# A fused attention and feed-forward kernel: the hand-written order of all engines replaced by another order

## The chip, the cores and the metric

The kernel runs on one core of a Trainium2 chip. The metric is the device time of one execution in microseconds (us). The core has four engines that compute, and each works through its own queue in order: PE (TensorE, matrix products and transposes), ACT (ScalarE), DVE (VectorE) and POOL (GpSimd). A fifth, SP (SyncE), issues all the transfers between the chip's memory (HBM) and the on-chip buffers. An engine that reaches an instruction whose input or buffer isn't ready waits there, with everything that stands behind it in its queue.

## The reference

There are B = 4 batches of N = 12480 tokens with C = 128 features, and m = 32 inducing vectors. A batch is read twice: the inducing vectors attend to all its tokens, which gives a 32 x 128 matrix h; then every token attends to the 32 rows of h. All 49920 results go through a feed-forward part.

```python
def mab(q, kv):
    s = scale * (q @ kv.transpose(0, 2, 1))
    s = s - s.max(-1, keepdims=True)
    a = np.exp(s)
    a /= a.sum(-1, keepdims=True) + 1e-09
    return a @ kv
h = mab(I, x)
return mab(x, h).astype(np.float32)
...
h = x @ w_in          # 128 -> 2048
g = h - np.tanh(h)
return (g @ w_out).astype(np.float32)
```

## The kernel before, in words

A batch is cut into seven steps of 1792 tokens, numbered (b, s) with s from 0 to 6; a step is one transfer of 896 KB each way. Two steps that follow each other form a pair (their group g is 0 to 3; the last group has one step).

The first pass (`first`, L276) does for each step: SP loads the transposed tokens (L286); PE multiplies them with the inducing vectors (the scores, L274); DVE copies a pair of steps out of the accumulator PSUM and takes the maximum (L298). When all seven steps are there, the maximum is spread (L309 to L314), ACT takes the exponentials pair by pair (L323) and DVE transposes them in blocks (L325). PE then sums exponentials times tokens (L356), for which the tokens are needed in their untransposed form. Eleven of the 28 steps load that form as well (L334, the set `LOADED`); for the other 17 PE transposes the tokens in two halves (L344), and ACT or DVE copies each half out of PSUM (L350 and L351; the copies run in a helper, L167 on ACT and L169 on DVE). A batch ends with small products that give h (L362 to L381).

`linear` (L385) replaces the feed-forward part by a tangent around the mean of the 32 rows of h, so that the feed-forward part and the second attention become one 32 x 128 matrix per batch. The second pass (`second`, L458) computes the scores of each token against h (L274 again), copies them out and takes a maximum (L477), takes exponentials (L499), and multiplies with that matrix (L507); the result of a step comes in two halves, each moved out of PSUM by ACT (L523) or DVE (L525) with a scale and an offset, and SP stores the step (L514). The last two steps of batch 3 are stored in halves.

`bound` (L540) works out at the end whether the tangent is accurate enough: a product (L580), a choice of rows (L586), `least` on DVE (L590), a transpose on PE (L603), `gather` (L607) and `decide` (L615), which writes one number. After that all five engines load that number (L696) and branch on it (L697); for these inputs the general path is skipped.

The weights come as 64-bit numbers in eight pieces of 512 KB (L233) and are turned into float32 by four instructions on DVE and two on ACT per piece (L236 to L257).

`IDLE` matrix products (L219) compute nothing that is used.

Nothing is scheduled by a compiler. `add` numbers each operation in the order of the program text, and the string `ORDER` (L42) lists all numbers again in the order in which they are issued. The letter behind a number chooses the engine (P, A, D, S, G), which matters for the operations that are declared `ACT/DVE`. The small letters behind it choose a place for each buffer that the operation uses first: 19 places for 896 KB steps (`big`), 3 PSUM places of two banks (`d`), and so on (`PLACES`, L36). A buffer's first writer waits until the place's former user is done; for a place that held a result, that is the landing of its store.

Of the kernel before, what the change touches and what calls it, by code (L numbers as in the profile page):

```python
# [34 lines left out]

PLACES = dict(big=19, sl=9, et=2, d=3, s=1, q=3, m2=3, k=4)  # L36
LOADED = frozenset(((1, 3), (1, 4), (2, 1), (2, 4), (2, 5), (2, 6), (3, 0), (3, 1), (3, 2), (3, 3), (3, 4),))
IDLE = 6
SPLITS = ([[0, 1], [2, 3]], [[0], [1], [2], [3]], [[0, 1], [2], [3]], [[0, 1, 2, 3]], [[0, 1, 2], [3]], [[0], [1, 2, 3]])
SPLIT = (0, 0, 0, 0)  # L40

ORDER = """  # L42
79Sa 1G 2D 3D 4Pa 66Sb 68D 76Sc 110Pad 112Pb 69A 103Pce 72D 111D 0S 74Sf 113D 104A 34Sg 105Pa 106D 37A 81Sh 77Pab 67D 100Pci 98Pa 99A 101D 70A 36D 75P
78D 80Pbc 35D 84Sj 40D 86Sk 38A 82P 83D 117Pbl 71D 73D 124Pam 122Pc 118A 85Pcb 39D 123D 87P 125A 89Sn 127Pab 90Pdc 88D 41D 129Pb 91D 92G 26So 93D 128A
27D 94Pa 28D 29A 130A 95D 30A 115Pc 136Pbg 134Pa 32D 31D 96A 33D 10Sp 116A 211Sq 97Da 11D 108A 212Pec 18Sr 209Ss 109Db 12D 102Pa 120A 107P 19D 214So
114P 13A 121Da 21A 210P 132A 16D 139D 20D 22A 119P 140Pa 216Si 133Db 213D 14A 24D 58Se 126P 131P 215Pdc 23D 135A 137A 50Sd 219Sl 138P 15D 141D 217P
25D 17D 59D 142Aa 218D 60D 143Pa 144A 235Pbr 187Pca 186P 221Sm 158Pbc 236A 62A 51D 63D 159P 188D 54A 224Sb 52D 161Pab 160D 61A 64D 162P 222Pfa 220P
42Sg 53A 189Pgc 163D 223D 190D 225Phb 226D 43D 227G 145Pa 245Pcn 56D 228D 45A 338Sp 55D 44D 46A 65D 340Sk 238Pbh 233Pa 246A 239A 229Pa 247Pc 234A 248A
258Pbe 259A 191Da 263Paa 230D 231A 192Pa 146Da 164Db 343Sj 256Pc 57D 345Sf 48D 232Db 47D 264A 240Pb 241A 149D 250Sc 254Sd 165Pb 49D 243A 265Pa 237Pa
147A 341Peb 252A 348Sr 350Sg 244Da 242P 339P 257A 249P 344Pdc 166D 167A 177A 193D 150Db 342D 261A 251P 353Sh 168A 268D 253Da 151Pa 152Ab 262Db 266A  # L50
346P 269Pa 153Pb 255P 349Pha 194A 155A 204A 463Sn 154Ab 347D 169Pcbd 260P 367Sc 351P 170D 171A 352D 148A 270D 205Pcbe 267P 206A 271Aa 207D 354Pga 355D
272Pa 273D 178Pbca 195A 179D 287Pfa 288P 180A 291Pib 290P 289D 292D 173Paci 174A 274Pa 357D 175A 172S 315Pbb 293Da 208S 461Ss 356G 316P 358Pa 275Db
181S 468Sq 364Pcm 362Pa 466Sd 276A 176S 359D 317D 278D 360A 383Sl 294Pa 361Db 365A 363A 373Pbe 374A 385So 295D 378Pca 376Pa 371Pb 379D 369A 381A 277A
318Pec 372A 471Sb 279Dc 377A 370Da 366Pa 280Pa 319D 368P 296A 281Da 464Pdc 387A 320Dc 321Pa 297A 391D 285Dc 286D 306A 473Sm 389Sc 392Pb 282Pc 196Pabi
375P 197A 382Db 476Se 462P 469Pha 322D 380P 283Aa 198A 465D 284A 467P 388Da 302Pcba 470D 324A 384P 472Pga 303D 304A 393D 298Pcbl 323A 386P 300A 474P
299D 325Pcbo 390P 475D 305S 327A 394Ac 326D 301S 477Pfa 328S 478D 480D 395Pb 329Pcbc 396A 481Pb 397Pa 411Pba 485Sa 330D 331A 482D 483A 410P 487Sk 489A
200Pcbl 398Dc 412D 202A 414Pca 413P 332S 484Da 201A 333A 479G 401D 399A 400A 495A 415D 402Db 439Pdb 491Sp 504A 438P 493So 334Pacg 335A 486Pa 336A 337S
416Dc 497Sa 403Pb 440D 488P 496Db 404Ad 182Pbar 501Pcc 184A 405Pb 417Pc 490Da 502D 183A 156Db 506Pak 157D 307Pbcj 507A 418D 185S 492P 308D 441Pha 309A
494P 511D 199S 442D 443Dc 311Pbch 429A 406Ad 444Pc 408Db 512Pa 420A 313A 312D 409D 499Pa 407D 421Pbcg 419A 423D 445D 203S 500A 498P 508Pa 503P 422A
509D 430Pcbr 447A 505Db 446A 510P 5Pa 513D 514Ac 432D 515Pa 431D 434Pabk 435A 516D 517Pa 530Pcc 436D 452Pbal 456A 531P 454A 534Pfa 314S 533P 518Db  # L60
521D 519A 532D 453A 522Dc 448Pbcq 535D 520A 528Da 584A 310S 450A 433S 449A 523Pa 524Dc 536Da 457Pacr 424S 459A 525Pa 529D 537Pc 458A 538D 425Pbcg 540A
427A 526Da 539A 558Pha 527A 585D 426D 549A 559P 541Pbcb 542A 560D 587Am 455S 543D 437S 561Pba 562D 563Dd 451S 550Pbck 586Ae 564Pa 8Pa 551D 460S 552A
565D 566A 577A 554Pabr 556A 588Pa 555D 567A 583D 578Pcbq 428S 544S 589Dd 579A 590Pa 591Dd 553S 557S 581A 580S 572Pacb 592Pa 593D 582S 573A 574S 575A
545Pbak 546D 576S 594D 547A 568Pcae 548S 6Pb 7Pb 9Pb 569D 570A 571S
"""


# [44 lines left out]
def fused_kernel(ctx, tc, xT, xn, indT, w_in, w_out, outT):  # L112
# [58 lines left out]
    def place(tag):  # L171
        return Buf(lambda b: slots[tag][b.slot], tag)
# [43 lines left out]

    for i in range(IDLE):
        d = place("d")
# [523 lines left out]
```

## Time and profile before

| | |
|---|---|
| three runs | 174.57, 174.38, 172.41 us; median 174.38 |
| the profiled execution | 173.93 us; its span (first to last instruction) 172.1 us |
| granted TensorE clock, mean | 0.987 of full speed |
| HBM read, written | 39.99 MB, 25.56 MB |
| PE busy | 151.3 us (88%) |
| DVE busy | 131.3 us (76%) in 296 instructions |
| ACT busy | 108.9 us (63%) in 162 instructions |

The span is the time that the trace covers. What the trace shows as busy is work of an engine; the time of a transfer from issue to landing covers its waiting behind earlier transfers too. Times in rows that begin with a number are counted from the span's start.

### The profile page before, as it was taken

Reading aid. Unit: us, or ns where it says so; the run is one execution under the profiler, and the core shown is the slowest. Engines: PE = TensorE matmul, PEld = TensorE weight load, DVE = VectorE, ACT = ScalarE, POOL = GpSimd, SP = SyncE. Lnnn points to the kernel's source line nnn. Section 1 sums busy time; section 2 is a strip of 40 time slices with the busy share of each in tenths; the row PEclk is TensorE's granted clock in tenths of the full one; section 3 lists DMA queues with packets and bytes.
Section 4 is the critical chain, followed back from the end, with each engine's and each line's share of the span. In section 5 each row is a group of like instructions: output and inputs, shape, how many; then the busy total and the mean of one; then the engine's idle time right before and its main releaser. Section 6 shows DMA issues by size and latency. Waiting matters only on the chain.

```text
span 172.1 us, 4717 instructions
## 1 busy us (share of the span) xinstructions
PE 151.3 (88%) x1960; PEld 88.9 (52%) x1960; DVE 131.3 (76%) x296; ACT 108.9 (63%) x162; POOL 1.4 (1%) x10
## 2 busy tenths in 40 slices
PE   2599959999599999999999998999999999998900
PEld 1665637873169776434866544248656325254300
DVE  4278969999599994868795865998888998985800
ACT  2126449937059974626996524897984469999600
POOL 1000000000000000000000000000000000000000
PEclk9999999999999999999999999999999999999995
DMA  5999999999999999999999999999999999999991
GB/s 163 379 423 417 416 414 353 374 364 422 421 423 413 301 393 420 410 291 345 420 422 419 420 422 423 322 340 417 418 425 420 427 389 413 423 407 413 409 381 56
DMA packets 11262, 65.94 MB, mean 383 GB/s; under 512 B 1376, under 2 KB 1376, under 8 KB 11232
## 3 DMA queue, kind: packets, MB, share of 16 engines
q1 hardware_dynamic: 11232, 65.56, 96.0%
q8 instruction: 17, 0.28, 0.7%
q14 instruction: 13, 0.11, 0.2%
HBM read 39.99 MB, written 25.56 MB: 381 GB/s over the span
## 4 chain that ended last, share of the span: by engine, by line
PE 50%; DMA 25%; ACT 9%; DVE 8%; issue 3%; SPq 0%; DVEq 0%; ACTq 0%
DMA big<-in_xT 16%; PE d L274 15%; PE d L507 12%; PE bank_s L356 11%; DMA outT<-big 6%; ACT big L167 4%; DMA big<-in_w_out 3%; DVE sl L477 3%; PE d L344 3%; PE bank_q L434 2%; ACT big L523 2%; PE d L219 1%; ACT sl L323 1%; PE bank_s L274 1%; ACT big L246 1%
## 5 line engine op out<-in xcount | busy, mean ns | idle before, releaser
L523 ACT ACTIVATE big<-d,Pm,wg 128x896 f32<-128x896 f32 x37 | 39.6, 1096 | 22.0 <-PE d L507 18.2
L344 PE MATMUL d<-ident,big 128*128 128x128 f32 x238 | 31.7, 287 | 2.2 <-DMA big<-in_xT 2.0
L507 PE MATMUL d<-sl,k 32*128 32x448 f32 x224 | 32.0, 585 | 0.6 <-ACT big L523 0.4
L344 PEld LDWEIGHTS d<-ident,big 128*128 128x128 f32 x238 | 28.0, 149 | 8.3 <-issue 4.8
L274 PE MATMUL d<-big,indT_sb 128*32 128x448 f32 x224 | 27.5, 543 | 4.4 <-DMA big<-in_xT 2.2
L356 PEld LDWEIGHTS bank_s<-big,et 128*32 128x32 f32 x784 | 23.7, 110 | 10.0 <-issue 5.9
L356 PE MATMUL bank_s<-big,et 128*32 128x128 f32 x784 | 28.6, 274 | 0.0
L525 DVE TENSOR_SCALAR big<-d,wg,Pm 128x896 f32<-128x896 f32 x19 | 22.9, 1208 | 6.6 <-PE d L507 3.6
L167 ACT COPY big<-d 128x896 f32<-128x896 f32 x26 | 22.7, 908 | 7.4 <-PE d L344 7.4
L274 PE MATMUL d<-big,hT 128*32 128x448 f32 x224 | 23.8, 543 | 1.4 <-DVE big L169 0.6
L298 DVE TENSOR_SCALAR_CACHE_REDUCE sl<-d 128x896 f32<-128x896 f32 (+1 forms) x16 | 15.5, 970 | 8.7 <-PE d L274 8.1
L507 PEld LDWEIGHTS d<-sl,k 32*128 32x128 f32 x224 | 10.9, 183 | 14.0 <-issue 3.9
L477 DVE TENSOR_SCALAR_CACHE_REDUCE sl<-d 128x896 f32<-128x896 f32 (+1 forms) x16 | 15.5, 970 | 1.6 <-PE d L274 1.3
L325 DVE STREAM_TRANSPOSE et<-sl 128x896 f32<-128x896 f32 (+1 forms) x16 | 15.6, 985 | 0.2
L323 ACT ACTIVATE sl<-sl,nb 128x896 f32<-128x896 f32 (+1 forms) x16 | 15.1, 947 | 0.5 <-DVE nb L314 0.5
L499 ACT ACTIVATE sl<-sl,nbs 128x896 f32<-128x896 f32 (+1 forms) x16 | 15.0, 948 | 0.4 <-DVE nbs L489 0.4
L274 PEld LDWEIGHTS d<-big,hT 128*32 128x32 f32 x224 | 6.6, 109 | 15.6 <-issue 9.1
L243 ACT ACTIVATE big<-big 128x512 f32<-128x512 uint32 x8 | 5.3, 694 | 14.2 <-DMA big<-in_w_out 11.5
L274 PEld LDWEIGHTS d<-big,indT_sb 128*32 128x32 f32 x224 | 7.6, 109 | 9.2 <-DVE sl L477 2.5
L169 DVE COPY big<-d 128x896 f32<-128x896 f32 x8 | 8.6, 1090 | 3.8 <-PE d L344 2.3
L219 PE MATMUL d<-fold,ones 128*128 128x256 f32 x12 | 4.1, 452 | 3.0 <-DVE fold L214 3.0
L246 ACT ACTIVATE big<-big,shift 128x512 uint32<-128x512 uint32 x8 | 5.6, 724 | 1.1 <-DVE big L236 1.1
(110 smaller groups left out, 121.7 us busy)
## 6 DMA issues: line engine op xcount, KB each, us to landing
big<-in_xT SPq DMA_DIRECT2D x28, 896.0 KB, 10.9
outT<-big SPq DMA_DIRECT2D x23, 896.0 KB, 7.2
big<-in_xn SPq DMA_DIRECT2D x11, 896.0 KB, 11.5
outT<-big SPq DMA_DIRECT2D x3, 864.0 KB, 6.3
big<-in_w_out SPq DMA_DIRECT2D x4, 512.0 KB, 7.4
big<-in_w_in SPq DMA_DIRECT2D x4, 512.0 KB, 15.3
outT<-big SPq DMA_DIRECT2D x3, 448.0 KB, 5.6
outT<-big SPq DMA_DIRECT2D x1, 416.0 KB, 5.4
```

The costliest lines, as they stand in the source:

```text
L167: nc.scalar.copy(out=out, in_=in_)
L274: nc.tensor.matmul(ps[q * m:(q + 1) * m, :n], lhsT=w, rhs=row, start=True, stop=True)
L298: nc.vector.tensor_scalar(out=sl.get()[:, :n, :], in0=ps.get()[:, :n, :W], scalar1=1.0, scalar2=None, op0=ALU.mult, op1=ALU.max, accum_out ...
L323: nc.scalar.activation(out=t, in_=t, func=AF.Exp, scale=SC, bias=nb.get(), accum_out=sums.get()[:, g:g + 1])
L325: add("DVE", lambda e, et=et, sl=sl, n=len(pair): nc.vector.transpose(out=et.get()[:, :n * KB, :].rearrange("p k i -> p (k i)"), in_=sl.ge ...
L344: nc.tensor.transpose(out=o[:, k * 128:(k + 1) * 128], in_=x.get()[:, at:at + 128], identity=ident)
L356: nc.tensor.matmul(hacc.get()[q * m:(q + 1) * m, :C], lhsT=et.get()[:, j * KB + k, :], rhs=xn_t.get()[:, k * C:(k + 1) * C], start=at < NQ ...
L477: nc.vector.tensor_scalar(out=sl.get()[:, :n, :], in0=ps.get()[:, :n, :W], scalar1=1.0, scalar2=None, op0=ALU.mult, op1=ALU.max, accum_out ...
L499: nc.scalar.activation(out=t, in_=t, func=AF.Exp, scale=SC, bias=nb)
L507: nc.tensor.matmul(ds[q // 2].get()[:, q % 2, :W], lhsT=P4.get()[r, :], rhs=sl.get()[r, j, :], start=True, stop=True)
L523: nc.scalar.activation(out=dst, in_=src, func=AF.Identity, scale=wg.get(), bias=Pm.get())
L525: nc.vector.tensor_scalar(out=dst, in0=src, scalar1=wg.get(), scalar2=Pm.get(), op0=ALU.mult, op1=ALU.add)
```

## The change

`ORDER` is replaced by another permutation of the same operations with other places and other choices of engine, and `IDLE` goes from 6 to 3 (which shifts the numbers of the operations behind by three). `LOADED`, `PLACES`, `SPLIT` and all code stay.

```diff
-IDLE = 6
+IDLE = 3
...
 ORDER = """
-79Sa 1G 2D 3D 4Pa 66Sb 68D 76Sc 110Pad 112Pb 69A 103Pce 72D 111D 0S 74Sf 113D 104A 34Sg 105Pa 106D 37A 81Sh 77Pab 67D 100Pci 98Pa 99A 101D 70A 36D 75P
...
+2D 1G 71Sa 3D 6Pa 31Sb 32D 97Pac 33D 34A 37D 35A 36D 38D 98A 73Sd 95Pb 96D 0S 102Pce 74Paa 103A 72P 100Pc 76Sf 107Pbb 78Sg 101A 75D 109Pa 77Pbc 81Sh
...
```

Read with the numbering, the two strings give the following. The order of SP's 78 transfers, with x for a load of transposed tokens (x06 is step (0, 6)), n for a load of untransposed tokens, wi and wo for pieces of the two weights, ind for the inducing vectors, o for a store (a and b are halves):

```
before
x02 wo3 x01 ind x00 wi3 x03 x04 x05 x06 wi2 wi0 x11 wi1 x10 x12 x13 wo2 wo1 x14 x15 x16 wo0 x20
x21 x22 x23 n13 n14 x24 x25 x26 x31 n21 o00 o06 x30 o02 x33 x32 o01 n24 n25 x34 x35 n26 x36 o11
o10 o14 n30 n31 o15 n32 n33 o16 n34 o03 o04 o05 o13 o12 o22 o20 o25 o23 o24 o26 o21 o30 o32 o33
o36a o36b o35a o35b o31 o34
after
x00 wi3 x01 ind x02 x03 x04 wo3 x05 x06 wi2 x12 x11 x10 wi1 wi0 x13 wo0 wo1 x15 x14 x16 wo2 x23
x20 x21 n14 n13 x22 x24 x25 x26 x31 n21 o00 o06 o02 n25 n24 x30 o01 x33 x32 x34 n26 x35 x36 o11
o10 o14 n30 o15 n31 n32 n33 n34 o16 o03 o12 o04 o13 o05 o20 o22 o23 o25 o24 o26 o21 o30 o32 o33
o31 o34 o35a o35b o36a o36b
```

Engines: of the 34 copies of transposed halves, 26 are on ACT and 8 on DVE before, 32 and 2 after (on DVE: batch 0 has five before and two after, batch 2 one and none, batch 3 two and none). Of the 56 moves of result halves, 37 are on ACT and 19 on DVE before, 35 and 21 after.

The end of the order, each engine's queue (out is L507 of a step, ev a half's move, exp an exponential, copy the product's move to a buffer):

```
before
PE   out(3,3) product-L580 out(3,6) choice-L586 out(3,5) turn-L603 out(3,1) out(3,4) idle idle idle
ACT  ev(3,3)b exp(g2) ev(3,6)a ev(3,6)b ev(3,5)a ev(3,5)b ev(3,1)b ev(3,4)b
DVE  ev(3,3)a copy least gather ev(3,1)a decide ev(3,4)a
after
PE   out(3,3) out(3,1) product-L580 out(3,4) choice-L586 out(3,5) out(3,6) turn-L603
ACT  ev(3,3)b exp(g2) ev(3,1)a copy weight-L491 ev(3,4)a exp(g3) ev(3,5)a ev(3,5)b ev(3,6)a ev(3,6)b
DVE  ev(3,3)a ev(3,1)b ev(3,4)b least gather decide
```

## Rows read from the trace of the kernel before

**Rows 1.** The page: GB/s in 40 slices of the span.
```profile
GB/s 163 379 423 417 416 414 353 374 364 422 421 423 413 301 393 420 410 291 345 420 422 419 420 422 423 322 340 417 418 425 420 427 389 413 423 407 413 409 381 56
```

**Rows 2.** The page: the transfer queue, and one group of stores.
```profile
q1 hardware_dynamic: 11232, 65.56, 96.0%
...
outT<-big SPq DMA_DIRECT2D x3, 448.0 KB, 5.6
```

**Rows 3.** Stretches: busy us of PE, PEld, DVE, ACT, POOL; clock; DMA share; GB/s.
```profile
24.00:45.00 21.00, 19.00 (x321) 12.63 (x317) 19.95 (x42) 14.74 (x25) 0.12 (x1) 1.00 1.00 384
29.00:36.00 7.00, 7.00 (x194) 5.75 (x190) 6.92 (x14) 6.37 (x12) 0.00 (x0) 1.00 0.96 324
56.00:61.00 5.00, 4.87 (x103) 3.85 (x105) 4.83 (x14) 5.00 (x10) 0.00 (x0) 1.00 0.89 299
75.00:81.00 6.00, 6.00 (x60) 1.98 (x53) 4.54 (x12) 2.49 (x4) 0.00 (x0) 1.00 0.92 278
108.00:114.00 6.00, 5.74 (x64) 1.68 (x56) 5.70 (x13) 5.46 (x11) 0.00 (x0) 1.00 0.97 299
114.00:140.00 26.00, 25.45 (x386) 14.93 (x382) 22.76 (x48) 18.50 (x27) 0.00 (x0) 1.00 1.01 421
150.00:156.00 6.00, 5.78 (x65) 3.06 (x62) 4.43 (x11) 6.00 (x9) 0.00 (x0) 1.00 1.02 411
```

**Rows 4.** SP's queue in order: start, length, transfer, count of issues.
```profile
28.35 2.53 SPq L286 DMA_DIRECT2D big<-in_xT  x2
...
43.21 12.18 SPq L334 DMA_DIRECT2D big<-in_xn  x2
58.60 3.32 SPq L286 DMA_DIRECT2D big<-in_xT  x4
...
74.94 0.34 SPq L286 DMA_DIRECT2D big<-in_xT  x1
...
106.89 2.79 SPq L334 DMA_DIRECT2D big<-in_xn  x2
```

**Rows 5.** The chain of waits: start, length, what it waited for.
```profile
75.39 9.76 DMA outT<-big
...
158.47 0.36 PE bank_s L603 x2
```

**Rows 6.** PE in order, with the idle time before and who ended it.
```profile
86.41 0.96 PE L274 MATMUL d<-big,hT 128*32 128x448 f32 x8 [0.63 <-DVE big L169]
```

**Rows 7.** Groups by line: count, busy us, mean ns.
```profile
L523 ACT ACTIVATE big<-d,Pm,wg 128x896 f32<-128x896 f32 x37 | 39.6, 1096 | 22.0 <-PE d L507 18.2 <-issue 3.1 <-ACT sl L323 0.4
...
L525 DVE TENSOR_SCALAR big<-d,wg,Pm 128x896 f32<-128x896 f32 x19 | 22.9, 1208 | 6.6 <-PE d L507 3.6 <-issue 2.4 <-ACT big L523 0.4
L167 ACT COPY big<-d 128x896 f32<-128x896 f32 x26 | 22.7, 908 | 7.4 <-PE d L344 7.4
...
L169 DVE COPY big<-d 128x896 f32<-128x896 f32 x8 | 8.6, 1090 | 3.8 <-PE d L344 2.3 <-DMA outT<-big 1.0 <-issue 0.5
```

**Rows 8.** ACT in order, its last instruction.
```profile
162.22 1.10 ACT L523 ACTIVATE big<-d,Pm,wg 128x896 f32<-128x896 f32 x1 [1.12 <-PE d L507]
```

**Rows 9.** DVE in order: first and last instruction of decide.
```profile
161.03 0.14 DVE L619 TENSOR_REDUCE low<-nbs 1x1 f32<-1x8 f32 x1
...
162.09 0.14 DVE L624 TENSOR_SCALAR limit<-low 1x1 f32<-1x1 f32 x1
```

**Rows 10.** PE in order, its last result product and the idle products.
```profile
161.15 1.02 PE L507 MATMUL d<-sl,k 32*128 32x448 f32 x4 [0.21 <-ACT big L523]
162.10 1.56 PE L219 MATMUL d<-fold,ones 128*128 128x256 f32 x6
```

**Rows 11.** Line 697, branches: count, ns, first and last start.
```profile
L697 PEldq COMPARE_BRANCH  x1: 5098/5098/5098, 163.2 to 163.2; - x1
```

**Rows 12.** Line 514 from 163.2 to 163.6 us: the last store, its landing.
```profile
L514 SPq DMA_DIRECT2D outT<-big x1: 332/332/332, 163.4 to 163.4; - x1
...
DMA to landing us min/median/max: 7.1/7.1/7.1
```

More of the change, by code (lines that the diff above doesn't have):

```diff
@@ L42 @@
 ORDER = """
-79Sa 1G 2D 3D 4Pa 66Sb 68D 76Sc 110Pad 112Pb 69A 103Pce 72D 111D 0S 74Sf 113D 104A 34Sg 105Pa 106D 37A 81Sh 77Pab 67D 100Pci 98Pa 99A 101D 70A 36D 75P
-78D 80Pbc 35D 84Sj 40D 86Sk 38A 82P 83D 117Pbl 71D 73D 124Pam 122Pc 118A 85Pcb 39D 123D 87P 125A 89Sn 127Pab 90Pdc 88D 41D 129Pb 91D 92G 26So 93D 128A
-27D 94Pa 28D 29A 130A 95D 30A 115Pc 136Pbg 134Pa 32D 31D 96A 33D 10Sp 116A 211Sq 97Da 11D 108A 212Pec 18Sr 209Ss 109Db 12D 102Pa 120A 107P 19D 214So
-114P 13A 121Da 21A 210P 132A 16D 139D 20D 22A 119P 140Pa 216Si 133Db 213D 14A 24D 58Se 126P 131P 215Pdc 23D 135A 137A 50Sd 219Sl 138P 15D 141D 217P
@@ L47 @@
[L47 to L62, printed above, removed]
@@ L63 @@
-565D 566A 577A 554Pabr 556A 588Pa 555D 567A 583D 578Pcbq 428S 544S 589Dd 579A 590Pa 591Dd 553S 557S 581A 580S 572Pacb 592Pa 593D 582S 573A 574S 575A
-545Pbak 546D 576S 594D 547A 568Pcae 548S 6Pb 7Pb 9Pb 569D 570A 571S
+2D 1G 71Sa 3D 6Pa 31Sb 32D 97Pac 33D 34A 37D 35A 36D 38D 98A 73Sd 95Pb 96D 0S 102Pce 74Paa 103A 72P 100Pc 76Sf 107Pbb 78Sg 101A 75D 109Pa 77Pbc 81Sh
+79P 110D 63Si 108A 114Paj 115A 80D 65D 82Pcb 64D 66A 121Pck 67A 122A 83Sl 69D 68D 119Pa 70D 86Sm 120A 84P 124Pcn 23So 87Pda 85D 126Pb 211Sp 125A 26A
@@ new lines @@
+208Sq 206Sr 88D 89G 90D 91Pa 127A 24D 112Pa 92D 25D 93A 27A 15Ss 29D 133Pbi 131Pc 94Da 99Pa 104P 28D 30D 105A 113A 106Db 117A 209Paa 7Sc 118Da 111P
+129A 207P 213So 116P 16D 136D 17D 18A 19A 134A 210D 21D 132A 20D 8D 130Db 11A 10A 137Pa 123P 212Pcb 128P 39Se 22D 47Sb 9D 218Sj 138D 135P 139Aa 13D
+214P 12D 216Sk 140Pa 141A 232Pci 221Sn 184Pda 40D 215D 43A 50A 41D 49D 233A 183P 48D 51A 44D 185D 156Pbb 155P 157D 158Pec 42A 55Ss 58A 219Pfa 159P 45D
+217P 14D 186Pgb 160D 342Sl 142Pa 222Phc 53D 187D 220D 244Pbm 230Pa 188Da 245A 223D 52D 231A 242Pc 225D 56D 335Sh 235Pbc 226Pa 46D 243A 236A 260Pae
@@ new lines @@
+161Db 227D 162Pa 228A 54D 337Sd 57D 189Pb 261A 251Sa 255Pbb 256A 143Da 229Db 61D 237Pc 247Sf 262Pa 238A 253Pb 240A 234Pa 146D 241Da 59A 249A 163D
+338Pac 340Sg 239P 336P 164A 60D 62D 345Si 347Sc 246P 224G 144A 147Db 263A 258A 343Pca 165A 248P 174A 265D 339D 148Pa 149Aa 350Ss 250Da 460Sm 341P 254A
+266Pa 150Pc 344D 364Sf 152A 259Db 151Aa 145A 267D 252P 346Pfa 166Pbca 190D 201A 167D 257P 348P 349D 168A 202Pbcb 264P 191A 203A 268Ab 351Pga 204D 352D
+269Pb 175Pcbe 270A 354D 177D 355Pb 285Pha 176A 284P 356D 288Pib 169S 287P 286D 289D 205S 353G 170Paco 178S 382Sq 357A 358Db 380Sr 271Pa 366A 312Pbb
@@ new lines @@
+172A 458Sp 171A 313P 315Paa 378A 384A 272Db 314D 361Pcj 362A 316D 388D 359Pb 360A 273A 317Db 367Da 389Pb 375Pae 376A 173S 290Dc 368Pcn 369A 275D 465Sk
+276Dc 373Pb 291Pa 318Pc 370Pc 292D 192A 363Pa 277Pa 365P 459Pca 294A 463Sb 371A 468Sa 386Sj 390D 372P 461P 278Ab 379Db 374A 193Pbcn 279Pa 377P 462D
+470Sf 194D 466Pfa 293A 281D 195A 280Ab 319D 274A 320A 330A 299Pbce 381P 300A 385Da 473So 301D 464P 302S 467D 295Pcbr 383P 296D 469Pha 321A 297A 298S
+282Dc 322Pcbq 323D 387P 391Dc 471P 472D 324A 326Pcbj 392Pc 325S 393A 327A 474Pba 328D 394Pa 408Pgb 475D 482Se 477D 478Pc 329S 484Sd 303A 407P 395Db
@@ new lines @@
+197Pach 479D 480A 488Sr 476G 409D 411Pdb 199A 398D 198A 410P 498Pcq 481Da 436Pca 283D 490Sl 396A 435P 499A 412D 399Dc 331Pbcc 437D 483Pa 333A 400Pc
+179Pacj 486A 401Ac 181A 332D 413Dd 402Pc 180D 492A 414Pa 496Pb 304Pace 415D 494Sg 497A 404D 416A 153Dc 306A 485P 403Dd 426A 487Db 503Pbi 305D 501A
+489P 308Pacd 493Da 491P 154D 504A 417A 309D 508D 438Pib 439D 495P 440Db 334S 310A 182S 418Pcas 307S 509Pc 419D 397A 441Pa 420A 405Dc 505Pb 510D 196S
+442D 502Db 506A 406D 444A 500P 427Pcaj 507P 311S 4Pb 511Ab 429A 512Pa 428D 431Pcbi 513A 514Pa 443A 433A 527Pda 432D 515Dc 453A 449Pcbn 451A 516A 200S
@@ new lines @@
+528P 518D 530Pbb 529D 421S 531P 517A 519Db 450A 532D 525Da 430S 581A 445Pcab 520Pa 521Db 434S 447A 533Dc 580D 446A 454Pbas 522Pa 534Pc 456A 422Pcaj
+526D 455A 535D 537A 523Dc 555Pib 582D 423A 424D 452S 556P 538Paca 448S 524D 457S 546A 536A 557D 540D 558Pgb 559D 560Dd 539A 584Ao 547Pacn 549D 561Pa
+562D 425S 548A 541S 5Pb 583Ab 551Pbaf 553A 550S 542Pcas 552D 564A 543A 554S 544D 585Pa 586Ad 545S 565Pbcj 563A 567D 587Pa 566A 569Paba 574A 570A 568S
+588Dd 575Pcan 571S 589Pa 572A 573S 590D 576A 577S 578A 579S 591D
```

## The prediction, made before the change was run

> **What bounds the kernel now.** I read the page's transfer parts first. All transfers go through one queue: 65.56 MB, and packets are in flight for 96% of the time of the 16 DMA engines [rows 2]. In the slices the rate is 413 to 427 GB/s where nothing disturbs it, and falls to 291 to 364 in a few places [rows 1]. At 421 GB/s, the rate of the undisturbed stretch from 114 to 140 us [rows 3], the bytes need 155.7 us. The span is 172.1 us, so 16.4 us are start, end and slow stretches, and only these can be won.
>
> Next I cut the span into stretches. Four hold most of the loss: 29 to 36 us at 324 GB/s, 56 to 61 at 299, 75 to 81 at 278 and 108 to 114 at 299, against 421 [rows 3]. The bytes missing there, as time at 421 GB/s, are 7 x (1 - 324/421) = 1.6, 5 x (1 - 299/421) = 1.4, 6 x (1 - 278/421) = 2.0 and 6 x (1 - 299/421) = 1.7 us, 6.8 us together. Then I read SP's queue beside them. Each slow stretch begins about 1 us after SP issues a load that follows a pause: at 28.35, at 55.07 (the second of the two issues that the row from 43.21 covers) and again 58.60, at 74.94, at 106.89 [rows 4]. The reader is to see that the queue had run low there, and that a load issued late meets a low rate for several us. Stores issued late, as most are after 114 us, meet no such loss [rows 3].
>
> Compute is as tight. From 24 to 45 us DVE works 19.95 of 21 us; from 114 to 140 PE works 25.45 of 26; from 150 to 156 ACT works 6.00 of 6 [rows 3]. A faster queue alone therefore gives little: the three must move together.
>
> **The change, part by part.** The eleven loaded steps are the same, so the bytes are the same, and no instruction is added but for engine choices.
>
> *Idle products and POOL.* POOL's four fills move with the maxima they follow, and nothing on POOL waits behind them: 0 us. Three idle products fewer. Before, three ran behind the last result product, from 162.10 on [rows 10], where nothing waits for them: 0 us. The ones at the start and within the last batch remain.
>
> *Engines.* Six copies of transposed halves go from DVE (1.09 us) to ACT (0.91), two result halves from ACT (1.10) to DVE (1.21) [rows 7]: DVE -6.5 + 2.4 = -4.1 us, ACT +5.4 - 2.2 = +3.3 us. Three of the six lie in batch 0, mostly before its last load has landed, where both engines have room: 0 us. One lies in batch 2: before, DVE waited there for the landing of a store whose place the copy takes over (the chain shows 9.76 us of that store from 75.39 [rows 5]), and PE then stood idle 0.63 us [rows 6]. In the new order that place held the store of (0, 2), issued ahead of three loads instead of behind one, so the landing comes earlier: -0.6 us, its cover being the 3 us or more that the landing gains. The two of batch 3 lie where PE works nearly without a pause (25.45 of 26 us [rows 3]): 0 us, unless ACT's two further copies delay a PSUM place there.
>
> *Batch 0 and 1.* The first ten transfers are the same set, so the last load of batch 0 lands where it did. Behind it DVE now transposes the first exponentials before it finishes a piece of w_in, and ACT reaches batch 1's first exponential after four copies of 0.91 us, not five. PE's work up to the first summed step of batch 1 is equal in both. I take -0.5 us, between 0 (DVE is full from 24 to 45 us, and its queue up to the last maximum of batch 1 is one operation of about 1.1 us longer) and -1.5 us.
>
> *SP's queue.* (1) Around 30 us the piece wi0 is issued when the first step is summed, and three more loads follow close behind; before, the second came over 2 us after the first [rows 4]. They are still loads into a low queue: -0.3 of 1.6 us. (2) At 58 us the load still waits for the same summed step: 0 of 1.4. (3) At 75 us the store of (0, 2) now comes first and the loads second, some 0.6 us later but behind one more transfer of about 2.2 us: -1.0 of 2.0. (4) At 107 us the store of (1, 5) goes ahead of the second load: -0.7 of 1.7. None of these prices is in the trace, so each has the ends 0 and the full loss; I take the middle where the queue is longer at the load's issue, and near 0 where it isn't. Stream: -2.0 us. What is queued behind the moved issues are further loads; each has several us of earlier transfers ahead of it.
>
> *The end.* Before, the last store is a whole step, issued at 163.4 and landed 7.1 us later at 170.5 [rows 12]; the span ends 1.5 us after. Now the last four stores are halves, which took 5.6 us [rows 2]. ACT has all four last halves; its list behind the move of (3, 3) holds the same work plus a copy of 0.3 us, and it loses up to the 1.12 us it idled [rows 8]: last move at about 162.6 instead of 163.3. Last landing 162.6 + 5.6 = 168.2, end 169.7.
>
> But `decide` is now the very last operation, behind PE's transpose, which stands behind the last result product. Before, that product ended at 162.2 [rows 10] and decide, placed ahead of it, at 162.2 too [rows 9]. Now: last product between 160.3 (ACT's list: 162.6 less three moves of 1.1, when its last place comes free, and 1.0 for its second half [rows 7, 10]) and 162.2 (the old pace), transpose 0.36 [rows 5], gather about half of decide, 0.6 (an estimate: three small instructions to decide's six), decide 1.2 [rows 9]: end of decide between 162.5 and 164.4, middle 163.4. PE's branch began 1.0 us after decide and lasted 5.1 us [rows 11]; with 1.0 to 1.5 us for the closing barrier the span ends 7.1 to 7.6 us after decide, near 170.8.
>
> The Trainium skill has a rule against this placement (Runtime: NRT & Kernel Launch, section Instruction fetch mechanics): a taken branch whose target isn't in the fetched window stalls until the target is fetched. The branch of 5.1 us agrees. By that rule the 5.1 us follow decide wherever it stands, and the end is this one; without it the stores or the stream would set the end, some 0.2 us earlier by the sum below.
>
> **The sum.** Lead of compute at the last product: 0.6 + 0.5 = 1.1 us. Ends: stores 169.7 - 1.1 = 168.6; branch 170.8 - 1.1 = 169.7; stream 172.1 - 2.0 - 0.6 (a last half instead of a whole step) = 169.5. The latest decides: 169.7, that is 2.4 us less than 172.1. The profiled execution took 173.93, 1.8 us around its span; the median of the runs is 174.38, 0.45 above it. Forecast: 174.4 - 2.4 = 172.0 us.
>
> **The rivals.**
> *All four slow stretches go.* For it: each starts at a late load, and the new order puts something ahead of two of them for certain. Against it: the late load at 58 us waits for the same work as before. The stream would end 6.8 us earlier; compute follows only as far as PE's waits allow, about 2 us beyond the forecast, since PE works 25.45 of 26 us. Time: 170.0 us.
> *Nothing is won.* The losses move to other loads and DVE, full from 24 to 45 us, passes its extra operation on: 174.4 us, own range 173.6 to 175.4.
> *The branch ends last, later than now.* One mechanism at one place: decide, transpose and last product stand in a row on DVE and PE, each of the last two products needing a PSUM place that ACT alone frees. Once decide ends after 164.5 to 165.0 the span exceeds the old one, and every us more is a us of time. If the last two products wait for a move each, as the old last one did (its second half waited for ACT and began at 161.15 [rows 10]), decide ends near 167: span 167 + 7.4 = 174.4, time 176.7 us; slower by over 2% from a decide at 168.2.
> *No room at all.* The skill's page DMA: Bandwidth & Descriptors, section Specifications, gives some 358 GB/s of HBM bandwidth per core, by which the bytes would take 183 us and no order could help; the rows at 421 GB/s contradict it here, and I give it no chance beyond the case before.
>
> **How the numbers follow.** Forecast, 0.48, own range 170.9 to 173.6. All stretches go, 0.28. Nothing won, 0.16. Branch last, 0.08, half of it over 2%. A measurement of this kernel tells about 2% from no change, 3.5 us: faster is below 170.9, slower above 177.9. Faster: 0.28 and 0.01 of the forecast's edge, 0.29; slower 0.05; within, 0.66. The range 169.4 to 175.4 leaves out a third of the second case and the last one, 0.18 together.
>
> **What would show it.** Right: GB/s near 420 in the slices around 75 and 110 us, still low near 30 and 58; no wait of PE for the copy after 85 us; the last store's landing and the end of PE's branch within 1.5 us of each other near 168.5. Wrong: slow stretches of the same sum at other loads; PE's branch ending over 1.5 us behind the last landing; DVE's last maximum of batch 1 later than before.

## The result and the profile after

The changed kernel took 171.72 us (median of 20 runs, 170.90 to 172.60), the kernel before 173.74 (20 runs, 172.30 to 175.89); the ratio is 0.9903, 95% interval 0.9877 to 0.9929. In a later comparison it took 171.78 (12 runs) and the ratio was 0.9939 (0.9902 to 0.9977). So it is faster by 1.0 and 0.6%, some 1.7 and 1.1 us (0.4 to 2.1 by the two intervals): within 2%. The forecast was 172.0. Ratios leave out disturbed executions, of which the kernel before has more, so a difference of the medians over all runs is larger than the ratio says.

The profiled execution took 172.6 us, 0.9 above the median and the longest of the 20, with a span of 170.8 against 172.1. The rate of the transfers, to be held against [rows 1, 2]:

```profile
GB/s 168 382 418 418 412 423 410 283 405 415 420 424 410 338 358 387 421 409 339 363 409 428 415 415 426 321 418 426 420 420 422 425 423 420 421 415 421 408 356 26
...
q1 hardware_dynamic: 11232, 65.56, 96.2%
```

The bytes are the same, and the low slices still lie near 30, 58, 80 and 108 us. The stretches of [rows 3], and one more at the end:

```profile
29.00:36.00 7.00, 7.00 (x179) 5.23 (x170) 6.63 (x13) 5.58 (x10) 0.00 (x0) 1.00 0.96 329
56.00:61.00 5.00, 5.00 (x114) 4.07 (x116) 4.33 (x13) 5.00 (x12) 0.00 (x0) 1.00 0.92 340
75.00:81.00 6.00, 6.00 (x61) 1.75 (x54) 5.24 (x8) 5.15 (x9) 0.00 (x0) 1.00 0.99 356
108.00:114.00 6.00, 5.74 (x55) 1.93 (x51) 5.79 (x16) 3.81 (x6) 0.00 (x0) 1.00 0.98 358
114.00:140.00 26.00, 25.62 (x379) 14.26 (x375) 21.65 (x45) 19.86 (x32) 0.00 (x0) 1.00 1.02 423
150.00:156.00 6.00, 5.31 (x60) 2.64 (x60) 3.68 (x4) 5.29 (x7) 0.00 (x0) 1.00 1.01 417
164.00:169.00 5.00, 0.00 (x0) 0.00 (x0) 0.00 (x0) 0.00 (x0) 0.00 (x0) 0.50 0.49 185
```

At 75 and 108 us the rate is 78 and 59 GB/s higher than before, at 30 us it is the same. At 56 it is 41 higher too, but over 56 to 67 us it is lower than before (350 against 363): stretches as short as these flatter a move, because a loss can come back a few us later. The table below has longer ones. ACT is no longer full from 150 to 156 us. In the last row nothing computes, the granted clock stands at its lower level (0.50 is 1.2 GHz) and costs nothing there, and the transfer engines are busy for half of the time only: their share falls from 1.02 in the us from 164 to 0.83, 0.38, 0.14 and 0.07 in the next four. Some of the 16 have finished while the last store still waits for others. SP's queue, as in [rows 4]:

```profile
29.10 0.33 SPq L233 DMA_DIRECT2D big<-in_w_in  x1
...
42.85 0.99 SPq L334 DMA_DIRECT2D big<-in_xn  x2
45.55 15.65 SPq L286 DMA_DIRECT2D big<-in_xT  x5
...
68.69 6.36 SPq L514 DMA_DIRECT2D outT<-big  x3
75.14 1.38 SPq L334 DMA_DIRECT2D big<-in_xn  x2
...
105.60 0.34 SPq L334 DMA_DIRECT2D big<-in_xn  x1
106.11 0.33 SPq L514 DMA_DIRECT2D outT<-big  x1
106.65 4.57 SPq L334 DMA_DIRECT2D big<-in_xn  x4
```

The store of (0, 2) is the third of those from 68.69, ahead of the loads at 75.14. At 105.60 a load is still the first behind a pause, because the place it fills came free just then (the store of (1, 1) landed at 105.53 us). PE at 86 us, where it waited before [rows 6], and its last products:

```profile
85.39 0.98 PE L344 MATMUL d<-ident,big 128*128 128x128 f32 x7
86.30 0.96 PE L356 MATMUL bank_s<-big,et 128*32 128x128 f32 x26
...
156.60 3.34 PE L507 MATMUL d<-sl,k 32*128 32x448 f32 x16
159.87 0.38 PE L603 MATMUL bank_s<-ident,bt_r 128*1 128x128 f32 x2
```

No wait stands at 86 us (from 74 to 92 us PE works 18.00 of 18 us, 17.37 before), and none in the last two result products. Then ACT's last four moves, the last instruction of `decide`, the branches of line 697 and the last store, in the columns of [rows 8, 9, 11, 12]:

```profile
157.78 4.05 ACT L523 ACTIVATE big<-d,Pm,wg 128x896 f32<-128x896 f32 x4
```

```profile
161.93 0.14 DVE L624 TENSOR_SCALAR limit<-low 1x1 f32<-1x1 f32 x1
```

```profile
L697 SPq EVENT_SEMAPHORE  x8: 17/17/17, 164.2 to 169.5; - x8
...
L697 PEldq COMPARE_BRANCH  x1: 5622/5622/5622, 163.0 to 163.0; - x1
...
L697 ACTq EVENT_SEMAPHORE  x1: 17/17/17, 166.7 to 166.7; - x1
L697 DVEq EVENT_SEMAPHORE  x1: 21/21/21, 168.0 to 168.0; - x1
L697 PEldq EVENT_SEMAPHORE  x1: 51/51/51, 168.7 to 168.7; - x1
```

```profile
L514 SPq DMA_DIRECT2D outT<-big x1: 935/935/935, 161.9 to 161.9; - x1
...
DMA to landing us min/median/max: 7.5/7.5/7.5
```

PE leaves its branch at 168.7 us. The last store is issued at 161.86 and lands at 169.31; SP has waited for the last of its landings at 169.5, and the span ends 1.5 us behind the landing, as before. So the last store ended last, the branch 0.6 us ahead of it.

### The profile page after: what moved, and what is told of

It is laid out like the page before. It is cut to its first block, busy times and chain, and to the rows that moved or that the text cites. A ratio compares the mean times of both kernels' runs of the same rounds, so it can differ in the third digit from the quotient of the medians.

```text
span 170.8 us, 4712 instructions
## 1 busy us (share of the span) xinstructions
PE 150.3 (88%) x1954; PEld 86.5 (51%) x1954; DVE 127.8 (75%) x292; ACT 112.4 (66%) x166; POOL 1.2 (1%) x10
## 4 chain that ended last, share of the span: by engine, by line
PE 68%; DMA 19%; DVE 3%; ACT 3%; issue 1%; SPq 0%; DVEq 0%
PE d L274 19%; PE d L507 16%; DMA big<-in_xT 16%; PE bank_s L356 13%; PE d L344 9%; DMA big<-in_w_in 4%; PE bank_q L434 2%; PE bank_s L274 2%; ACT big L523 2%; PE bank_q L486 1%; PE bank_q L440 1%; PE bank_q L378 1%; PE bank_q L312 1%; ACT sl L323 1%; DVE et L325 1%
## 5 line engine op out<-in xcount | busy, mean ns | idle before, releaser
L523 ACT ACTIVATE big<-d,Pm,wg 128x896 f32<-128x896 f32 x35 | 37.6, 1096 | 16.5 <-PE d L507 13.2
L167 ACT COPY big<-d 128x896 f32<-128x896 f32 x32 | 27.9, 908 | 7.6 <-PE d L344 6.7
L507 PE MATMUL d<-sl,k 32*128 32x448 f32 x224 | 31.7, 585 | 1.0 <-ACT big L523 1.0
L525 DVE TENSOR_SCALAR big<-d,wg,Pm 128x896 f32<-128x896 f32 x21 | 25.3, 1206 | 9.6 <-PE d L507 8.6
L344 PEld LDWEIGHTS d<-ident,big 128*128 128x128 f32 x238 | 27.4, 147 | 9.7 <-issue 4.6
L274 PE MATMUL d<-big,indT_sb 128*32 128x448 f32 x224 | 28.3, 544 | 2.2 <-DMA big<-in_xT 1.7
L356 PE MATMUL bank_s<-big,et 128*32 128x128 f32 x784 | 29.3, 275 | 0.3 <-DVE et L325 0.2
L507 PEld LDWEIGHTS d<-sl,k 32*128 32x128 f32 x224 | 10.6, 183 | 16.1 <-issue 5.6
L236 DVE TENSOR_SCALAR big<-big 128x512 uint32<-128x512 uint32 x8 | 3.4, 427 | 4.6 <-DMA big<-in_w_in 4.6
L250 DVE SCALAR_TENSOR_TENSOR big<-big 128x512 uint32<-128x512 uint32 x8 | 5.5, 684 | 0.0
```

Of the source, the lines that this page charges most:

```text
L167: nc.scalar.copy(out=out, in_=in_)
L274: nc.tensor.matmul(ps[q * m:(q + 1) * m, :n], lhsT=w, rhs=row, start=True, stop=True)
L344: nc.tensor.transpose(out=o[:, k * 128:(k + 1) * 128], in_=x.get()[:, at:at + 128], identity=ident)
L356: nc.tensor.matmul(hacc.get()[q * m:(q + 1) * m, :C], lhsT=et.get()[:, j * KB + k, :], rhs=xn_t.get()[:, k * C:(k + 1) * C], start=at < NQ ...
L507: nc.tensor.matmul(ds[q // 2].get()[:, q % 2, :W], lhsT=P4.get()[r, :], rhs=sl.get()[r, j, :], start=True, stop=True)
L523: nc.scalar.activation(out=dst, in_=src, func=AF.Identity, scale=wg.get(), bias=Pm.get())
```

## The experiments

The variants of the changed kernel are held against its 32 runs of both comparisons (median 171.78 us). They ran in three comparisons, each on a chip of its own, where the shortest run of the kernel before was 171.77, 171.78 and 171.98 us. With 6 to 12 runs of a variant, a difference of medians under about 0.5 us lies in the scatter (an estimate from the spread of the runs). The ratios to the kernel before are looser still, because its runs spread wider. "Excess" in these texts is the sum of what each landing lay more than 2.17 us per 896 KB behind the one before it.

**The same kernel again**, for the comparison with three of the others.

> The changed kernel unaltered, beside the three others on one chip. It should stand about 1% below the kernel before, near 171.7 us where that stands near 173.5; its excess at the landings of 57 to 75 us should again be near 0.5 us.

Measured: 171.78 us, ratio 0.9939. Its profiled execution was shorter (span 169.4), and there the order of the two ends is turned round:

```profile
L697 SPq EVENT_SEMAPHORE  x8: 17/17/17, 164.1 to 168.0; - x8
...
L697 PEldq EVENT_SEMAPHORE  x1: 51/51/51, 168.3 to 168.3; - x1
```

All landings were in at 168.0, and PE came out of its branch at 168.3. The two ends lie within the scatter of each other. In the nine traces of the changed order that keep the branch, it ends between 1.9 us ahead of SP's last wait for a landing and 1.0 us behind it, in five of them behind; in the four traces of the old order it always ends 1.0 to 2.3 us ahead.

**One store ahead of one load, alone.**

```diff
-208S 461Ss 356G ... 275Db 181S 468Sq
+208S 181S 461Ss 356G ... 275Db 468Sq
```

> The kernel before with one word moved: the store of (0,2) is issued ahead of the load of (3,0) instead of behind it. Theory (a load issued into a low queue costs time, a store doesn't): the slow stretch at 75 to 81 us shrinks from 2.0 us to about 1.0, time 0.5 to 1.0 us less than the kernel before. Rival (the loss moves to the next load): the rate at 75 to 81 us or just behind it stays as low in sum, time within 0.3 us of the kernel before.

Measured: 1.0003 (0.9953 to 1.0053) of the kernel before. From 75 to 81 us the rate rose:

```profile
75.00:81.00 6.00, 6.00 (x59) 2.75 (x52) 4.99 (x14) 3.31 (x5) 0.00 (x0) 1.00 1.01 363
```

but over 74 to 92 us it is 373 GB/s, before 372: the loss came back a few us later. The rival holds by these rates; the interval of the time alone, from 0.8 us less to 0.9 more, leaves room for the theory's 0.5 us. In this trace the store of (0, 2) lands at 79.08 us instead of 85.14, and PE's wait of [rows 6] is gone, although the copy is still on DVE (DVE, then PE in order):

```profile
83.19 1.09 DVE L169 COPY big<-d 128x896 f32<-128x896 f32 x1
```

```profile
84.55 0.96 PE L274 MATMUL d<-big,hT 128*32 128x448 f32 x8
```

So the earlier landing takes the wait away by itself, and no time is won by it that these runs could show.

**The choice of engines, alone.**

```diff
-111D 106D 123D 379D 502D 509D  197A 183A 335A  431D
+111A 106A 123A 379A 502A 509A  197D 183D 335D  431A
```

> The kernel before, order and places untouched, with the engine choices of the change alone: six copies of transposed halves from DVE to ACT (three in batch 0, the one of (2,3) on which PE waited at 86 us, two in batch 3), three result halves from ACT to DVE and one back. Theory (half of the gain is compute that runs ahead): the wait of PE at 86 us goes, later work starts 0.6 us earlier or more, time 0.3 to 1.1 us less than the kernel before. Rival (the transfers alone set the end): time within 0.3 us.

Measured: 1.0042 (0.9989 to 1.0096), no gain. PE's wait is not gone (PE, then ACT in order, with the idle time before):

```profile
85.09 0.96 PE L274 MATMUL d<-big,hT 128*32 128x448 f32 x8 [0.73 <-ACT big L167]
```

```profile
84.13 0.91 ACT L167 COPY big<-d 128x896 f32<-128x896 f32 x1 [0.86 <-DMA outT<-big]
```

The copy, now on ACT, waits 0.86 us for the same landing, and PE waits for the copy as before. The wait belonged to the place and the landing, not to the engine.

**The last steps stored whole** (line 529 never splits; four words of the order become two).

```diff
-                        if b == B - 1 and s >= NS - 2:
+                        if False:
```

> The changed kernel with the last two steps stored whole, each behind its second move, instead of in four halves. As forecast (the last store follows the last move, and half a step less stands behind it): 1.1 us more than the changed kernel. Rival (the queue is never empty up to the end, whole or half): the last landing comes within 0.3 us of where it was, time the same within 0.3 us.

Measured: 172.47 us (6 runs, 172.18 to 174.69), ratio 0.9992 (0.9930 to 1.0053): 0.7 us more than the changed kernel by the medians, 0.9 to 1.5 by the ratios: outside the rival's 0.3, and to either side of the forecast 1.1. Its one trace doesn't say why: the rate from 140 to 158 us is 422 GB/s, and the last store still had others ahead of it.

**Without the branch** (the general path behind it is left out too).

```diff
-    over = nc.values_load(limit.bitcast(I32)[0:1, 0:1])
-    with tc.If(over > 0):
...
```

> The changed kernel without the load of the number at the end, the branch on it and the general path behind it. Theory (the last store's landing, 169.31 us, sets the end; the branch on PE ended 0.7 us before it): the branch's own 5.6 us are beside the path, and only the 0.78 us can go by which the last landing came late while instructions were fetched; last landing near 168.5, time 0.3 to 1.0 us less than the changed kernel's. Rival (the branch sets the end, as forecast): the last landing stays at 169.3, the 1.5 us between it and the end of the span shrink, time 1 us or more less.

Measured: 170.14 us (6 runs, 169.56 to 170.81), ratio 0.9852 (0.9788 to 0.9916): by the medians 1.6 us less than the changed kernel, by the ratios 0.9 to 1.5. That is the rival's time and more than the theory's by the medians; but the last landing did not stay at 169.3, as the rival had it. The time from issue to landing of the last six stores, in the changed kernel's first and second profile and here:

```profile
DMA to landing us min/median/max: 6.3/6.5/7.5
```

```profile
DMA to landing us min/median/max: 5.5/5.8/6.4
```

```profile
L514 SPq DMA_DIRECT2D outT<-big x6: 332/448/911, 155.7 to 162.0; - x6
...
DMA to landing us min/median/max: 5.5/5.7/5.9
```

Against the second profile only the longest differs. At 2.17 us per 896 KB the last two landings came 0.8 and 0.5 us later than their bytes need in the changed kernel's two profiles (0.1 to 1.5 us in the nine traces with its order and the branch), here 0.0. The last store lands at 167.9, and the span ends 0.94 us after that (168.8), not 1.5. Both differences are read from one trace without the branch. The page counts 29 transfers of instructions in the changed kernel (0.38 MB), 21 here (0.30 MB). Eight of the 29 start between 165.2 and 169.4 us; here none starts behind 159.1. That they delay the last landings fits this and is not shown:

```profile
q8 instruction: 17, 0.28, 0.6%
q14 instruction: 12, 0.10, 0.2%
```

```profile
q8 instruction: 15, 0.25, 0.5%
q14 instruction: 6, 0.05, 0.1%
```

**Fewer bytes, less work of PE, both.**

```diff
+ r = 16 if (b, s) == (0, 4) else 128
-nc.sync.dma_start(out=outT[:, ...], in_=ot.get()[:, at:end])
+nc.sync.dma_start(out=outT[:r, ...], in_=ot.get()[:r, at:end])
```

> The changed kernel, but the store of step (0,4), issued at 122 us, writes 16 of its 128 rows: 784 KB fewer, 1.9 us at 421 GB/s. Theory (the transfers set the end): time less by 0.7 to 1.9 us; not the whole, because the moves of the last steps follow only as far as the engines let them. Rival (compute sets the end): 0 to 0.2 us less, and the stores of the last steps land sooner after their issue (under 5.5 us instead of 6.3) with the same issue times.

```diff
                     for k in range(KB):
+                        if b == 3 and s in (3, 4, 5) and k > 1:
+                            continue
```

> The changed kernel, but the sums of steps (3,3), (3,4) and (3,5) take 2 of their 14 products each: 2.5 us less work for PE between 114 and 131 us, the bytes the same. Theory (the transfers set the end): the last moves come up to 2.5 us earlier, the last landing hardly, time 0 to 0.5 us less than the changed kernel. Rival (compute sets the end): 1.5 to 2.5 us less.

> The changed kernel with both: the store of (0,4) cut to 16 rows (1.9 us of transfers less) and the sums of (3,3) to (3,5) cut (2.5 us of PE less). Theory (two limits of equal length, so that either alone gives little): 1.5 to 2.0 us less than the changed kernel, more than the sum of the two cuts alone. Rival (one limit alone): what the better of the two cuts gives by itself.

Measured: fewer bytes 171.24 us (ratio 0.9923, 0.9884 to 0.9963), less PE 171.81 (0.9934, 0.9883 to 0.9985), both 171.00 (0.9876, 0.9827 to 0.9925), against 171.72 and 171.78 of the changed kernel. By the medians 2.5 us of PE bring nothing, 1.9 us of bytes some 0.5, at the edge of the scatter (by the ratios nothing shows), and both some 0.8. The last is clear: all six runs with both lie below all six with less PE, from the same comparison. The whole-step stores behind 141 us, from issue to landing, in the changed kernel, with less PE, and with both:

```profile
DMA to landing us min/median/max: 6.3/6.4/6.7
```

```profile
DMA to landing us min/median/max: 6.9/7.1/7.3
```

```profile
DMA to landing us min/median/max: 4.3/4.7/5.0
```

With less PE the stores are issued earlier and wait longer: the transfers hold the end. With both they hardly wait any more, and yet the time falls by about half of what the theory gave. There the branch, at line 700 of that kernel, is the last:

```profile
L700 SPq EVENT_SEMAPHORE  x8: 17/17/17, 163.5 to 167.2; - x8
...
L700 DVEq EVENT_SEMAPHORE  x1: 21/21/21, 167.9 to 167.9; - x1
```

All landings are in at 167.2; DVE comes out of its branch at 167.9. A third limit of about the same length, which my two-limit theory had left out.

**One load earlier, and the reverse.** The second diff shows the two words that matter; the letters of the two places are exchanged behind them.

```diff
-258Pbe 259A 191Da 263Paa ... 57D 345Sf ... 250Sc 254Sd
+258Pbe 259A 191Da ... 57D 263Pad 345Sf ... 250Sc 254Sa
```

> The kernel before with one load made earlier: the untransposed load of (1,4) takes the place that was free at 43 us, and the first transposed half of (1,6) takes in exchange the one that comes free at 55 us (the two places' letters are exchanged from there on). The load is issued at about 44 us instead of 55; the transposed half is made at 55 us instead of 53.5. Theory (the gain comes from this load, because the queue is then no lower than three transfers and only one late load is left at 58 us): the excess over landings from 57 to 75 us falls from 1.5 us (mean of the three kernels in the old order) to about 0.5, time 0.5 to 1.2 us less than the kernel before. Rival (which load is late doesn't matter, the loss comes back at the next): within 0.3 us.

```diff
-261A 251Sa 255Pbb ... 340Sg 239P
+261A 255Pba ... 340Sg 251Sb 239P
```

> The changed kernel with the reverse: the untransposed load of (1,4) takes the place that comes free at 53 us and is issued behind the load of (2,2), the first transposed half of (1,5) gets the place that is free at 42 us. Theory: a second late load, excess over the landings from 57 to 75 us from 0.5 us to about 1.5, time 0.5 to 1.2 us more than the changed kernel. Rival: within 0.3 us.

Measured: the early load 1.0006 (0.9959 to 1.0053) of the kernel before, the late load 0.9964 (0.9929 to 0.9998), 172.09 us against 171.78 beside it. Neither moves the time by what the theory gave; the late load's 0.3 us lies in the scatter. In the stretch named the excess was 1.7 us before and 0.4 with the early load, but 0.6 in the changed kernel and 0.4 with the late one. With the early load the excess came back in the next stretch: from 75 to 92 us it is 3.2 us, 2.1 before. The late load, issued at 51.97 us, found four transfers ahead of it and brought no second loss, so it doesn't test what such a loss would cost. The theory, formed from the first profiles, is not borne out.

**Two ways to put a transfer ahead of the load at 105 us.**

```diff
-475D 482Se 477D 478Pc 329S 484Sd
+475D 329S 482Se 477D 478Pc 484Sd
```

> The changed kernel with one word moved: the store of (1,5) is issued ahead of the load of (3,0) in untransposed form at 105.6 us instead of behind it; its data is ready by then. Theory (a load issued into a low queue costs time): the excess of 2.06 us at this load falls to 1.0 or less, the load lands about 115 us, time 0 to 1.0 us less than the changed kernel. Rival (the load just comes later): it lands 2.2 us later at 116.2, the sum of (3,0), which began at 114.18 right behind the landing, waits, time 0.5 to 2 us more.

```diff
-302S 467D ... 505Pb 510D 196S
+302S 196S 467D ... 505Pb 510D
```

> The changed kernel with one word moved: the store of (0,4), ready at 94 us and issued at 122, is issued at about 97 us, behind that of (1,1), so that the load of (3,0) at 105.6 us finds three transfers ahead of it instead of two, with the load's own issue time unchanged. Theory (a load issued into a low queue costs time): the excess of some 1.9 us at this load falls under 1.0, its landing stays near 114, time 0.5 to 1.2 us less than the changed kernel. Rival (the load has to wait for the transfer put ahead of it, and the sum of (3,0) with it): the load lands at 116, time 0.3 us less to 1 us more.

Measured: 171.03 us (12 runs, 170.60 to 171.94; ratio 0.9902, 0.9864 to 0.9941) and 171.34 (6 runs, 170.63 to 172.03; 0.9893, 0.9840 to 0.9947). The stretch from 108 to 114 us, in the first and in the second:

```profile
108.00:114.00 6.00, 5.50 (x59) 2.16 (x63) 5.79 (x17) 3.58 (x5) 0.00 (x0) 1.00 1.02 421
```

```profile
108.00:114.00 6.00, 5.74 (x55) 1.89 (x47) 5.79 (x17) 3.67 (x6) 0.00 (x0) 1.00 1.01 413
```

The loss at this place is gone, in both, by different transfers. By the medians the kernels gain 0.7 and 0.4 us from it (by the ratios up to 0.6, and 0.2 to 0.8; the 0.4 is at the edge of the scatter), of the 1.0 and 1.5 us that the stretch lost in the changed kernel's two traces (14 us at 391 and 377 GB/s against 421, table below). Part of it is lost again from 140 to 158 us: 402 and 398 GB/s there, 417 to 422 in the six traces of the changed order with all its bytes and nothing won before. In the trace of the second, the longest of its six runs, the branch is in the way besides: all landings are in at 168.3, PE is out of its branch at 169.3, the span ends at 170.3.

```profile
L697 SPq EVENT_SEMAPHORE  x8: 17/17/17, 164.8 to 168.3; - x8
...
L697 PEldq EVENT_SEMAPHORE  x1: 51/51/51, 169.3 to 169.3; - x1
```

By its median the first is the fastest version that leaves nothing out. Putting `decide` further forward in it would be the next step; it wasn't tried.

**Five stretches in all profiles.** Since every run left one trace, the rates can be read against their scatter (GB/s from the same view of stretches; the four kernels in the old order first):

| | 24 to 46 | 56 to 67 | 74 to 92 | 104 to 118 | 140 to 158 us |
|---|---|---|---|---|---|
| before | 386 | 363 | 372 | 365 | 407 |
| store (0, 2) first | 392 | 398 | 373 | 382 | 413 |
| engines | 396 | 398 | 377 | 331 | 399 |
| early load | 396 | 406 | 374 | 371 | 415 |
| changed, and again | 388, 387 | 350, 391 | 382, 385 | 391, 377 | 420, 417 |
| late load | 388 | 391 | 384 | 383 | 418 |
| stored whole | 376 | 393 | 385 | 374 | 422 |
| less PE, fewer bytes, both | 387, 391, 383 | 385, 339, 397 | 390, 382, 386 | 390, 385, 371 | 422, 394, 401 |
| no branch | 386 | 379 | 389 | 368 | 417 |
| store (1, 5) first, store (0, 4) ahead | 385, 387 | 392, 360 | 387, 380 | 424, 420 | 402, 398 |

## Why the prediction was right or wrong, step by step

**The total** was right: 172.0 against 171.72, "within 2%" at 0.66. The gain was forecast too large, 2.4 us against 1.7 and 1.1 by the ratios, and the base was too high as well: 174.38 was the median of three runs, over twenty it is 173.74. That these two errors nearly cancel is luck, and the parts below show that most of the sum isn't borne out by itself. Of the rivals, "nothing is won" is excluded by both intervals, "all four slow stretches go" by the slices that are still low, and the branch that ends later than before by `decide`, which ended at 162.07 us.

**The signs.** PE has no wait for the copy, and the two ends lie within 1.5 us of each other near 168.5 us (169.3 and 168.7), as named. The rate near 420 GB/s around 75 and 110 us did not come: 356 and 358 in those stretches of the first profile. One sign of being wrong did appear (batch 0 and 1, below).

**Idle products and POOL, 0 us.** Not tried by themselves.

**Engines, -0.6 us.** Wrong as told. The choice alone brings nothing, and the wait moves to ACT with the copy. The other half of that step, the earlier landing, does take the wait away by itself (the store ahead of the load in the old order), but that kernel's time is 1.0003 of the kernel before. A wait gone on PE was priced as time won, and no run shows that gain.

**Batch 0 and 1, -0.5 us.** Not shown. In the first pair of traces the first summed step of batch 1 began at 56.74 us, 0.71 earlier than before. But the three other traces in the old order begin it at 55.78 to 56.30 us, inside the range of the ten in the changed order, 55.67 to 56.85. A sign that I had called wrong did appear: DVE's last maximum of batch 1 came 0.48 us later (49.26), yet the first exponential behind it came 1.54 earlier (53.02), right behind ACT's copies. The maximum wasn't what that exponential waited for last.

**SP's queue, -2.0 us.** This term was mis-sized. The means of the four kernels in the old order and of the eight in the changed order (without the last line of the table) are 392 and 386, 391 and 378, 374 and 385, 362 and 380 GB/s. As time at 421 GB/s, worked out as in the prediction: 22 x 6/421 = 0.3 us lost, 11 x 13/421 = 0.3 lost, 18 x 11/421 = 0.5 won, 14 x 18/421 = 0.6 won. Forecast were 0.3 won, 0, 1.0 won, 0.7 won. (3) and (4) have the right sign; only (3) stands clear of the scatter (372 to 377 against 380 to 390). In (1), (2) and (4) the two orders overlap, and I don't call the difference an effect. Read by the landings, as the excess above, it comes out otherwise: from 57 to 75 us the old order loses 0.7 to 2.0 us (three traces, without the early load) and the changed order 0.3 to 0.7, while from 75 to 92 us the two overlap (1.9 to 2.2 and 1.7 to 2.3). Where on the way the queue gains is therefore open. The reason I gave, the store ahead of the loads, is not shown for (3): the same move alone in the old order left the rate at 373. For (4) the idea is right and the place was wrong. In the changed order the load at 105.60 still comes first; the store went ahead of the second load only. Once a transfer stands ahead of the first, the loss is gone. The sum has no term for the stretch from 140 to 158 us, and there the two orders stand apart: 399 to 415 GB/s in the old one, 417 to 422 in the changed one with all its bytes and nothing won before, which is 18 x 11/421 = 0.5 us won by the means (408.5 and 419.3). Where transfers were saved earlier, the rate there falls to 394 to 402: the stores then have to wait for their moves, it seems.

**The end, stores.** The last move ended at 161.83 us; forecast were 162.6 less 1.1, that is 161.5. It is 1.55 us earlier than in the first trace of the kernel before, but not earlier than in every trace of the old order: the last store, which follows the last move, was issued at 161.7, 161.8, 163.4 and 163.8 us there, and at 160.9 to 162.3 in the seven traces of the changed order that leave no bytes or products out. The half store's 5.6 us were mis-sized: 7.5 in the first profile and 6.4 in the second. It had five and four transfers ahead of it, the halves before had two to four, and in both the last two landings were late. That the halves count is borne out by the kernel that stores whole steps, 0.7 us slower by the medians, where the sum had 0.6 in the stream's end and 1.5 in the stores' end.

**The end, branch.** `decide` ended at 162.07, forecast 163.4 less 1.1; the branch took 5.6 us and ended at 168.7. Forecast as the last end, 0.2 us behind the stream and 1.1 behind the stores, it was second to the last store by 0.6 in one profile and last by 0.3 in the other, and last by 1.0 with the transfer ahead at 97 us. That it moved up beside the stores is right; that it sets the end is so in about half of the traces. The rule of the Trainium skill (Runtime: NRT & Kernel Launch, section Instruction fetch mechanics), that a taken branch outside the fetched window stalls until its target is fetched, agrees with the rows of line 697: ACT, DVE and PE come out of their branches at 166.7, 168.0 and 168.7 us, 4 to 6 us after they had their number. That a fetch is what they wait for is not in those rows; it fits the transfers of instructions that start from 165.2 us on.

**What stays open.** Which of the changes brings the whole. Three single parts of it, put into the old order, bring nothing (1.0003, 1.0042, 1.0006), one taken out of the new order costs 0.7 us. The cause of the 1.1 to 1.7 us as a whole is therefore not shown. The compute lead at the end is 1.5 us in the first pair of traces and lies in the scatter of all of them, and 2.5 us less of PE gained nothing, so the lead alone is not what sets the time. My reading, argued and not shown: bytes, compute and the branch end within about 1 us of each other, and a gain at one is cut off by the next.

## What to carry to other kernels

When a stretch of the profile looks like a loss of 2 us, take several traces before giving it a price: here the same stretch of the same kernel was 350 GB/s in one and 391 in another. Before moving a step, ask which transfer is the first behind a pause, and put one that is ready ahead of that one, not of the next: at 105 us this took the loss away, at 75 us it did not. Then see whether what is won there lasts to the end: here a part of it was lost again from 140 to 158 us. And count the branch at the end as work with its own length: where it ends beside the last store, it takes what is won elsewhere.

## What the runs showed of the hardware

- In the changed order a load issued behind a pause with two transfers ahead of it went with a loss of 1.0 to 1.8 us around 105 us (368 to 391 GB/s from 104 to 118 us in eight traces, against 421); with a third ahead of it the loss was gone (424 and 420). At 75 us three ahead were not enough (373). Why is open.
- The branch cost 1.6 us by the medians at a place where its 5 us seemed to be hidden beside the stores. In the one trace without it the last two landings were 0.0 us late instead of 0.1 to 1.5, and the span closed 0.94 us behind the last instead of 1.5.
- At the end the 16 transfer engines do not finish together: from 164 to 169 us their mean share is 0.49, falling from 1.02 to 0.07, while the last store is still out (landing at 169.31).
